# Experts' input copies on ScalarE, and weight loads tied to VectorE's place in the pass

## The chip, the cores and the metric

The kernel runs on one core of a Trainium2 chip. The metric is the device time of one execution in microseconds. Before the change, three runs gave 418.44, 418.54 and 419.1 us; the median is 418.54.

A core has five engines, each with its own queue of instructions: TensorE (PE; its weight loads are shown apart as PEld), VectorE (DVE), ScalarE (ACT), GpSimd (POOL) and the sync engine (SP). Engines wait for each other on semaphores. Data moves between HBM and the on-chip SBUF by DMA; the sync engine and POOL issue most of the transfers here. Matmul results go to PSUM, from where ScalarE or VectorE move them to SBUF.

## What is computed

An attention block with a gated state, then a mixture of 16 experts in 4 groups. Cut to what matters:

```python
# attention, per batch (4), head (8), step (768), head width 48
f = 1 / (1 + exp(-f_logit))
state = f[t] * state + outer(k[t], v[t])
y[t] = q[t] @ state
# rows of all heads side by side: x is 3072 x 384
g_idx = argmax(x @ w_group)            # group of 4
e_idx = argmax(x @ w_expert[g_idx])    # expert of 4 in the group
h  = maximum(x[tokens] @ w1[g, e], 0)  # 384 -> 1024
ye = h @ w2[g, e]                      # 1024 -> 384
out[tokens] = (g_softmax * e_softmax)[:, None] * ye
```

Every token goes to one of the 16 experts, so the tokens of an expert must be gathered before its matmuls and scattered after them.

## The kernel before

**Two stages.** Up to about 130 us the kernel works on the attention block in 12 units and, as chunks of tokens are done, ranks the experts by their number of tokens. It starts with two "early" passes, of the two fullest experts, for the tokens known by then. From about 154 us it runs 16 expert passes. Pass 0 and pass 15 take 128 rows each (the rest of the two early experts' tokens); passes 1 to 14 take 230 down to 174 rows (`WIDTHS`), one expert each, fullest first. `PLACES` maps the number of a pass to a place in the ranking, and `who` (one row of integers, made by VectorE at line 300) holds the expert's number for each place.

**One pass.** POOL gathers its rows (`fetch`, line 404, one indirect DMA for each block of up to 128 rows). The rows are turned so that the model dimension lies on the partitions. That is done in one of two ways:
- `square_in` (line 426): VectorE turns 32x32 squares from SBUF to SBUF. Passes 2 to 14 use it.
- `turn_in` (lines 435 to 441): TensorE transposes into PSUM (`xg_ps`), and a copy moves the result into the tile `xe`. The two early passes use it, with the copy on ScalarE, and passes 0, 1 and 15, with the copy on VectorE.

Then `up` (line 450) multiplies with the first layer, and ScalarE applies the relu from PSUM to SBUF (line 451). `down` (line 486, or `down_rows` at 471 for 128 rows) multiplies with the second layer; ScalarE moves the result from PSUM (487), VectorE turns it back in `square_out` (433), ScalarE scales the rows (458) and POOL scatters them to the output (461).

**Order of work.** For TensorE, VectorE, ScalarE and the sync engine, the program's order is the order of execution (`manual_schedule`, line 85); POOL's order is left to the scheduler. In the loop at lines 964 to 991, iteration n issues `square_out` of pass n-1, `square_in` of pass n+2, `up` of pass n+1 and `down` of pass n. On TensorE the order is therefore up(0), up(1), down(0), up(2), down(1), up(3), down(2) and so on to up(14), down(13), down(14), up(15), down(15). Iteration 2 ends with `beyond`, some bookkeeping on VectorE; iteration 3 ends with `weakest` and `flags`, where VectorE waits for one transpose by TensorE.

**Weights.** Each expert has two layers of 1536 KB. `load_weights` (line 395) has the sync engine read the expert's number into a register (388) and then issue the loads of the first and of the second layer (392). There are three sets of weight buffers: pool `wq` has one, used by passes 1, 4, 7 and so on; pool `wp` has two. A load waits until the matmuls of the pass that had the buffer before are through: pass m uses the buffers of pass m-3. The call stands at the end of iteration n and loads pass n+3 (984 and 985). During the attention stage, `load_next` (819) copies the number to another tile, `who_late`, before it is read.

Of the kernel before, what the change touches and what calls it, by code (L numbers as in the profile page):

```python
# [11 lines left out]
I32 = mybir.dt.int32  # L12
# [6 lines left out]
P = 128  # L19
# [4 lines left out]
def kernel(  # L24
# [12 lines left out]
    nc = tc.nc  # L37
# [5 lines left out]
    GE = G * EG  # L43
# [25 lines left out]
    wp = ctx.enter_context(tc.tile_pool(name="wp", bufs=2))  # L69
# [7 lines left out]
    def const(shape, dtype, name):  # L77
        return cp.tile(shape, dtype, tag=name, name=name)

    def bank(shape, name):  # L80
        return ps.tile(shape, FP32, tag="bank", name=name)
# [189 lines left out]
    who = const([1, GE], I32, "who")  # L271
# [115 lines left out]
    def value(ap, top):  # L387
        return nc.values_load(ap, engines=(ET.SP,), min_val=0, max_val=top, skip_runtime_bounds_check_because="a table that the routing makes within these bounds")

    def load_layer(pool, e, layer):  # L390
        w = pool.tile([P, KO, F] if layer == 1 else [P, FO, DM], FP32, tag=f"w{layer}", name=f"w{layer}")
        nc.sync.dma_start(out=w, in_=(w1v if layer == 1 else w2v)[bass.ds(e, 1)].rearrange("o p k f -> (o p) k f"))
        return w

    def load_weights(pool, ap):
        e = value(ap, GE - 1)
        return load_layer(pool, e, 1), load_layer(pool, e, 2)

    def fetch(pool, rows, n, top=N, late=False):

        w = {"n": n, "pool": pool, "early": top < N, "late": late, "blocks": [(j, min(P, n - j * P)) for j in range((n + P - 1) // P)]}
        w["x"] = pool.tile([P, len(w["blocks"]), RW], FP32, tag="xg", bufs=2 if pool is ep else 6, name="xg")
        for j, m in w["blocks"]:
            nc.gpsimd.indirect_dma_start(out=w["x"][:, j, :], out_offset=None, in_=x_dram[0:1 + top, :], in_offset=bass.IndirectOffsetOnAxis(ap=rows[:, j:j + 1], axis=0))  # L404
        return w

    def room(w, shape, name):

        full = w["pool"].tile([P, shape, P if w["pool"] is ep else WIDE], FP32, tag=name, name=name)
        w[name[:2].replace("xe", "xT") + "_full"] = full  # L410
        return full[:, :, 0:w["n"]]
# [9 lines left out]
    def square_in(w):  # L421

        w["xT"] = room(w, KO, "xe")
        x = w["x"][:, :, 0:DM].rearrange("p j (o g c) -> p j g o c", o=KO, c=SQ)
        xT = w["xT_full"].rearrange("p o (j k c) -> p j k o c", j=2, c=SQ)
        squares(w, lambda n, k_, rk, g, rg: nc.vector.transpose(out=xT[rg, 0:n, k_], in_=x[rk, 0:n, g]))  # L426

    def square_out(w):

        w["rows"] = w["pool"].tile([P, 2, DM], FP32, tag="yr", name="yr")  # L430
        y = w["rows"].rearrange("p j (o g c) -> p j g o c", o=KO, c=SQ)
        yT = w["yT_full"].rearrange("p o (j k c) -> p j k o c", j=2, c=SQ)
        squares(w, lambda n, k_, rk, g, rg: nc.vector.transpose(out=y[rk, 0:n, g], in_=yT[rg, 0:n, k_]))  # L433

    def turn_in(w):
        w["xT"] = room(w, KO, "xe")
        for j, m in w["blocks"]:
            pt = bank([P, KO, P], "xg_ps")
            for ko in range(KO):
                nc.tensor.transpose(out=pt[:, ko, 0:m], in_=w["x"][0:m, j, ko * P:(ko + 1) * P], identity=ident[0:m, 0:m])  # L440
            (nc.scalar.copy if w["early"] else nc.vector.tensor_copy)(w["xT"][:, :, j * P:j * P + m], pt[:, :, 0:m])  # L441

    def up(w, w1):
        n = w["n"]
# [31 lines left out]
    def down(w, w2):  # L476
        n = w["n"]
        if n == P:
            for _ in down_rows(w, w2):
                pass  # L480
            return
        w["yT"] = w["yT_full"][:, :, 0:n]
        for m in range(KO):
            yp = bank([P, n], "yo")
            for fo in range(FO):
                nc.tensor.matmul(yp, lhsT=w2[:, fo, m * P:(m + 1) * P], rhs=w["h"][:, fo, :], start=(fo == 0), stop=(fo == FO - 1))  # L486
            nc.scalar.copy(w["yT"][:, m, :], yp)  # L487

    def scaled(w, settle=False):
        if w["n"] > P:  # L490
            for j, m in w["blocks"]:
                with settled(settle and j):
                    put(w, j, m, w["rows"][:, j, :])
# [22 lines left out]
    def early():  # L516

        ws = [fetch(ep, rows_e[:, p:p + 1], P, (CLOSE + 1) * B * P) for p in range(EARLY)]
        yield
        for w in ws:  # L520
            turn_in(w)
            yield
        for p, w in enumerate(ws):
            yield from up(w, weights[p][0])
        for p, w in enumerate(ws):
            yield from down_rows(w, weights[p][1])
# [380 lines left out]
    wq = main.enter_context(tc.tile_pool(name="wq", bufs=1))  # L907
# [3 lines left out]
    PLACES = [0] + list(range(EARLY, GE)) + list(range(1, EARLY))  # L911

    def pass_of(n):
        p = PLACES[n]
        if p < EARLY:
            return fetch(mo, rows_p[:, p, 1:2], P)
        return fetch(mo, rows_p[:, p, :], WIDTHS[p - EARLY])

    fari = const([1, 1], I32, "fari")

    def weakest():

        worst = const([P, 1], FP32, "worst")
        nc.vector.tensor_reduce(out=worst, in_=decays.rearrange("p c a n -> p (c a n)"), axis=AX, op=OP.min)
        wt = bank([1, P], "wt")
        nc.tensor.transpose(out=wt, in_=worst, identity=ident)
        far = const([1, 2], FP32, "far")
        nc.vector.tensor_reduce(out=far[:, 0:1], in_=wt, axis=AX, op=OP.min)
        nc.vector.tensor_scalar(far[:, 1:2], far[:, 0:1], math.exp(-SAFE), None, OP.is_lt)
        nc.vector.tensor_copy(fari, far[:, 1:2])  # L930

    def flags():

        nc.vector.tensor_copy(both[:, 0:1], fari)
        nc.vector.tensor_scalar(rest, b_end, 0, None, OP.is_gt)
        nc.vector.tensor_tensor(both[:, 1:2], fari, rest, OP.max)
# [4 lines left out]
    ahead = {n: load_weights(wq if n % 3 == 1 else wp, who[0:1, PLACES[n]:PLACES[n] + 1]) for n in range(1, 2)}  # L941
# [8 lines left out]
    def run_up(n):  # L950
        for _ in up(ws[n], ahead[n][0]):
            pass

    outs = [const_out(i) for i in range(2)]
    turn_in(ws[0])
    for _ in first[0]:
        pass
    opening = up(ws[0], ahead[0][0])
    next(opening)
    next(opening)  # L960
    turn_in(ws[1])
    for _ in opening:
        pass
    for n in range(GE - 1):
        w = ws[n]
        if n + 3 < GE:
            ws[n + 3] = pass_of(n + 3)
        if n == 0:
            ahead[2] = load_weights(wp, who[0:1, PLACES[2]:PLACES[2] + 1])
        past, coming = ws.pop(n - 1, None), ws.get(n + 2)  # L970
        if past and past["n"] > P:
            square_out(past)
        if coming and coming["n"] > P:
            square_in(coming)
        if n + 2 < GE:
            run_up(n + 1)
        if past:

            scaled(past, n == GE - 3)
        if coming and coming["n"] == P:  # L980
            turn_in(coming)
        w["yT_full"] = outs[n % 2]
        down(w, ahead.pop(n)[1])
        if n + 3 < GE:
            ahead[n + 3] = load_weights(wq if n % 3 == 1 else wp, who[0:1, PLACES[n + 3]:PLACES[n + 3] + 1])
        if n == 2:
            with tc.tile_pool(name="tb", bufs=1) as tb:
                beyond(False, tb)
        if n == 3:
            weakest()  # L990
            flags()
# [79 lines left out]
    with tc.If(more > 0), ExitStack() as late:  # L1071
# [5 lines left out]
        with tc.For_i(0, last, 1) as i:  # L1077
# [14 lines left out]
            w = fetch(ep, row, P, late=True)  # L1092
# [32 lines left out]
```

## Time and profile before

| | |
|---|---|
| median of three runs | 418.54 us |
| the profiled execution | 417.84 us |
| its span, from the first to the last instruction | 416.0 us |
| mean granted TensorE clock | 0.994 |
| up(0), 128 columns, 48 matmuls | starts at 154.73 us |
| up(1), 230 columns, 48 matmuls | 164.32 us, takes 11.24 us |
| down(1), 230 columns, 48 matmuls | 189.56 us, takes 9.48 us |
| last matmul of down(15) ends | about 410.5 us |
| a weight layer, from issue to landing | 6.6 to 13.5 us, median 7.2 |
| line 441 on VectorE, four copies | 467 to 558 ns |
| line 441 on ScalarE, two copies | 479 and 480 ns |
| line 388, register load on the sync engine | 263 to 277 ns |

How to read the profile: it is one execution. Times are counted from the start of the span. A line of a timeline has a start, a length, the engine, the source line, the operation, the tile written and the tiles read, the shape and the number of like instructions merged; in brackets stand the engine's idle time before it and what ended that. A busy TensorE is one that has matmuls in its pipeline. "issue" stands for idle time in which nothing that the profile shows was waited for, "remote" for a release whose source was not found.

### The profile page before, as it was taken

The numbers are of one execution on the slowest core, as the hardware profiler recorded it, in microseconds if no ns is written. First come the engines' busy times: TensorE is split into PE (matmuls) and PEld (weight loads), VectorE is DVE, ScalarE is ACT, GpSimd is POOL, SyncE is SP. The second block draws the span as 40 slices with busy tenths as digits, with TensorE's granted clock in tenths as the row PEclk, the third lists the DMA queues.
The fourth block names the chain that finished last, engine by engine and source line by source line (L and its number), as shares of the span: only waits on it lengthen the run. The fifth ranks groups of instructions, "written<-read, shape, count | busy, mean of one in ns | idle before, by whom it ended". The sixth has DMA issues, their size and how long they took to land.

```text
span 416.0 us, 10268 instructions
## 1 busy us (share of the span) xinstructions
PE 404.0 (97%) x4143; PEld 371.9 (89%) x4143; DVE 264.3 (64%) x783; ACT 162.2 (39%) x365; POOL 85.7 (21%) x132
## 2 busy tenths in 40 slices
PE   8999999999999997999999999999999999999994
PEld 3888888888888966989999999999999999999992
DVE  6666878787998702440799767485595595584230
ACT  6777878887664211211223122222231232232220
POOL 5000010101040174001041221311321230120230
PEclk9999999999999999999999999999999999999999
DMA  9999987879869499855729467586495596485010
GB/s 191 208 216 197 201 179 147 164 159 289 244 225 378 163 337 345 318 179 184 271 84 335 137 245 265 164 315 208 170 348 169 217 352 200 173 318 162 28 48 24
DMA packets 132146, 88.99 MB, mean 214 GB/s; under 512 B 102582, under 2 KB 122748, under 8 KB 132090
## 3 DMA queue, kind: packets, MB, share of 16 engines
q1 hardware_dynamic: 125666, 75.50, 60.6%
q0 software_dynamic: 5792, 11.92, 9.5%
q10 hardware_dynamic: 632, 0.83, 0.6%
q8 instruction: 35, 0.57, 0.6%
q14 instruction: 21, 0.17, 0.1%
HBM read 78.71 MB, written 9.83 MB: 213 GB/s over the span
## 4 chain that ended last, share of the span: by engine, by line
PE 48%; issue 30%; DMA 9%; POOL 6%; DVE 3%; POOLq 1%; another core or an unknown queue 1%; ACT 1%; SPq 0%; ACTq 0%; DVEq 0%
PE hp L450 12%; PE yo L486 6%; DMA out_dram<-yt,xg 6%; PE yo L471 4%; PE cs L616 4%; POOL out_dram L461 4%; PE ap L704 3%; PE y L746 3%; POOL xg L404 2%; PE x_ps L795 2%; PE tr_q L650 2%; PE tr_k L650 2%; PE y L742 2%; PE ap L689 2%; PE y L754 2%
## 5 line engine op out<-in xcount | busy, mean ns | idle before, releaser
L450 PE MATMUL hp<-xe,w 128*128 128x128 f32 (+14 forms) x864 | 141.3, 323 | 2.6 <-issue 1.8
L450 PEld LDWEIGHTS hp<-xe,w 128*128 128x128 f32 x864 | 137.4, 192 | 4.5 <-issue 2.4
L486 PE MATMUL yo<-h,w 128*128 128x230 f32 (+13 forms) x672 | 115.8, 333 | 0.0
L433 DVE STREAM_TRANSPOSE yr<-yT 32x192 f32<-32x192 f32 (+1 forms) x208 | 70.5, 339 | 70.5 <-ACT yT L487 67.9
L486 PEld LDWEIGHTS yo<-h,w 128*128 128x128 f32 x672 | 113.7, 190 | 0.2
L451 ACT ACTIVATE h<-hp 128x256 f32<-128x256 f32 (+14 forms) x72 | 34.2, 478 | 109.1 <-PE hp L450 100.2
L426 DVE STREAM_TRANSPOSE xe<-xg 32x192 f32<-32x192 f32 (+1 forms) x208 | 69.6, 335 | 8.7 <-PE hp L450 5.8
L461 POOL DMA_INDIRECT out_dram<-yt,xg x32 | 34.5, 1078 | 156.1 <-ACT yt L458 150.5
L487 ACT COPY yT<-yo 128x230 f32<-128x230 f32 (+13 forms) x42 | 13.5, 325 | 80.5 <-PE yo L486 80.5
L404 POOL DMA_INDIRECT xg<-x_dram,rows_p x30 | 29.6, 986 | 51.1 <-DMA out_dram<-yt,xg 25.7
L471 PE MATMUL yo<-w,h 128*128 128x384 f32 x64 | 21.3, 486 | 0.0
L707 DVE TENSOR_TENSOR am<-ap,tri 128x512 f32<-128x512 f32 x24 | 15.1, 688 | 7.3 <-PE ap L704 7.3
L616 PE MATMUL cs<-ld_f,tri 128*128 128x384 f32 x48 | 18.5, 505 | 0.5 <-POOL blank L177 0.3
L471 PEld LDWEIGHTS yo<-w,h 128*128 128x128 f32 x64 | 11.9, 190 | 7.4
L458 ACT ACTIVATE yt<-yr,xg 128x384 f32<-128x384 f32 (+13 forms) x26 | 14.4, 604 | 5.4 <-DVE yr L433 5.4
L623 POOL DMA_DIRECT2D ends<-eq x10 | 5.4, 542 | 52.2 <-ACT eq L617 52.2
L692 DVE TENSOR_TENSOR am<-ap,seen 128x384 f32<-128x384 f32 x24 | 12.2, 551 | 5.5 <-PE ap L689 5.5
L757 ACT COPY xT<-y 128x512 f32<-128x512 f32 x24 | 13.4, 587 | 5.0 <-PE y L746 4.4
L651 ACT COPY Tk<-tr_k 128x512 f32<-128x512 f32 x24 | 15.2, 636 | 0.0
L651 ACT COPY Tq<-tr_q 128x512 f32<-128x512 f32 x24 | 15.0, 625 | 0.4 <-PE tr_q L650 0.3
L441 DVE COPY xe<-xg_ps 128x384 f32<-128x384 f32 (+1 forms) x4 | 2.1, 535 | 20.5 <-remote 9.7
L650 PE MATMUL tr_q<-ident,qh 128*128 128x128 f32 x96 | 14.5, 274 | 0.5 <-issue 0.5
(187 smaller groups left out, 448.4 us busy)
## 6 DMA issues: line engine op xcount, KB each, us to landing
w<-in_moe_w_dram SPq DMA_DIRECT2D x34, 1536.0 KB, 7.2
qh<-in_q_dram SPq DMA_DIRECT2D x12, 384.0 KB, 6.1
ld_k<-in_k_dram SPq DMA_DIRECT2D x12, 384.0 KB, 4.4
v<-in_v_dram SPq DMA_DIRECT2D x12, 384.0 KB, 5.4
ld_f<-in_f_logit_dram SPq DMA_DIRECT2D x11, 384.0 KB, 5.5
x_dram<-x_kept SPq DMA_DIRECT2D x2, 1536.0 KB
x_dram<-x POOLq DMA_DIRECT2D x2, 384.0 KB
x_dram<-x ACTq DMA_DIRECT2D x2, 384.0 KB, 7.4
```

The lines of the kernel that those rows point to most:

```text
L404: nc.gpsimd.indirect_dma_start(out=w["x"][:, j, :], out_offset=None, in_=x_dram[0:1 + top, :], in_offset=bass.IndirectOffsetOnAxis(ap=rows ...
L426: squares(w, lambda n, k_, rk, g, rg: nc.vector.transpose(out=xT[rg, 0:n, k_], in_=x[rk, 0:n, g]))
L433: squares(w, lambda n, k_, rk, g, rg: nc.vector.transpose(out=y[rk, 0:n, g], in_=yT[rg, 0:n, k_]))
L450: nc.tensor.matmul(hp[:, o, :], lhsT=w1[:, ko, (f + o) * P:(f + o + 1) * P], rhs=w["xT"][:, ko, :], start=(ko == 0), stop=(ko == KO - 1))
L451: nc.scalar.activation(h[:, f:f + 2, :], hp, AF.Relu)
L461: sent = nc.gpsimd.indirect_dma_start(out=out, out_offset=bass.IndirectOffsetOnAxis(ap=w["x"][0:m, j, DM + 1:RW].bitcast(U32), axis=0), in ...
L471: nc.tensor.matmul(yp, lhsT=w["h"][:, fo, :], rhs=w2[:, fo, :], start=(fo == 0), stop=(fo == FO - 1))
L486: nc.tensor.matmul(yp, lhsT=w2[:, fo, m * P:(m + 1) * P], rhs=w["h"][:, fo, :], start=(fo == 0), stop=(fo == FO - 1))
L616: nc.tensor.matmul(cs.rearrange("t h d -> t (h d)"), lhsT=tri, rhs=nl[:, b], start=True, stop=True)
L650: nc.tensor.transpose(out=pt[:, a, :], in_=w[nm + "h"][:, b, 2 * a:2 * a + 2, :].rearrange("t r d -> t (r d)"), identity=ident)
L651: nc.scalar.copy(w["T" + nm][:, b], pt)
L707: nc.vector.tensor_tensor(am[:, r], ap[r], tri.unsqueeze(1).broadcast_to((P, HP, P)), OP.mult)
```

## The change

First, the copy at the end of `turn_in`: ScalarE does it always, except in the block at the end of the program that handles tokens beyond the passes' widths (`late`). Second, the load of the weights: the call moves from the end of iteration n, for pass n+3, to the beginning of iteration n, for pass n+2, ahead of that iteration's `square_out` and `square_in`. VectorE copies the expert's number to a new tile, `who_next`, and the sync engine reads it from there. Pass 2's load, in iteration 0, stays as it is; the pools are the same for each pass.

```diff
-            (nc.scalar.copy if w["early"] else nc.vector.tensor_copy)(w["xT"][:, :, j * P:j * P + m], pt[:, :, 0:m])
+            (nc.vector.tensor_copy if w["late"] else nc.scalar.copy)(w["xT"][:, :, j * P:j * P + m], pt[:, :, 0:m])
...
+    who_next = const([1, GE], I32, "who_next")
...
         past, coming = ws.pop(n - 1, None), ws.get(n + 2)
+        if 0 < n < GE - 2:
+            p = PLACES[n + 2]
+            nc.vector.tensor_copy(who_next[:, p:p + 1], who[:, p:p + 1])
+            ahead[n + 2] = load_weights(wq if n % 3 == 2 else wp, who_next[0:1, p:p + 1])
         if past and past["n"] > P:
             square_out(past)
...
         down(w, ahead.pop(n)[1])
-        if n + 3 < GE:
-            ahead[n + 3] = load_weights(wq if n % 3 == 1 else wp, who[0:1, PLACES[n + 3]:PLACES[n + 3] + 1])
```

## The prediction

> **What bounds the kernel now.** I read three views: busy time by engine and by slice, then each engine's timeline around the places the change touches, then the same stretch cut into 5 us windows.
>
> ```profile
> PE 404.0 (97%) x4143; PEld 371.9 (89%) x4143; DVE 264.3 (64%) x783; ACT 162.2 (39%) x365; POOL 85.7 (21%) x132
> PE   8999999999999997999999999999999999999994
> ```
>
> TensorE is busy 404.0 of 416.0 us, and the slices show one dip in the middle, in slice 16 (about 156 to 166 us), where the first expert pass starts. Here are TensorE, ScalarE, VectorE and one issue of the sync queue in that place, each from its own timeline:
>
> ```profile
> 157.41 0.76 PE L440 MATMUL xg_ps<-ident,xg 128*128 128x128 f32 x6
> 158.00 1.97 PE L450 MATMUL hp<-xe,w 128*128 128x128 f32 x16
> 160.37 0.48 PE L450 MATMUL hp<-xe,w 128*128 128x128 f32 x2 [0.40 <-issue]
> 161.08 0.27 PE L450 MATMUL hp<-xe,w 128*128 128x128 f32 x1 [0.22 <-issue]
> 162.48 1.08 PE L450 MATMUL hp<-xe,w 128*128 128x128 f32 x5 [1.14 <-issue]
> 164.32 11.24 PE L450 MATMUL hp<-xe,w 128*128 128x230 f32 x48 [0.76 <-ACT h L451]
> ...
> 158.36 0.39 ACT L451 ACTIVATE h<-hp 128x256 f32<-128x256 f32 x1 [2.85 <-PE xg_ps L440]
> 163.23 0.94 ACT L451 ACTIVATE h<-hp 128x256 f32<-128x256 f32 x3 [4.48 <-remote]
> ...
> 163.28 0.94 DVE L441 COPY xe<-xg_ps 128x384 f32<-128x384 f32 x2 [9.67 <-remote]
> 164.14 5.70 DVE L426 STREAM_TRANSPOSE xe<-xg 32x192 f32<-32x192 f32 x16
> 175.60 5.71 DVE L426 STREAM_TRANSPOSE xe<-xg 32x192 f32<-32x192 f32 x16 [5.76 <-PE hp L450]
> ...
> 163.59 3.71 SPq L392 DMA_DIRECT2D w<-in_moe_w_dram  x1
> ```
>
> TensorE had run 16 matmuls of up(0) in 1.97 us, then needs from 160.0 to 163.6 for the last eight. ScalarE and VectorE both wake within 0.05 us of each other at 163.2, although the matmuls they need were issued by 158.2. I call this the stall. Only then does up(1) start.
>
> ```profile
> 155.00:160.00 5.00, 4.97 (x46) 4.78 (x44) 0.00 (x0) 0.90 (x2) 3.78 (x5) 1.00 1.04 328
> 160.00:165.00 5.00, 2.40 (x11) 1.89 (x12) 1.69 (x5) 0.94 (x3) 1.26 (x2) 0.99 1.00 338
> 165.00:170.00 5.00, 5.00 (x19) 4.54 (x18) 4.67 (x14) 0.56 (x1) 0.00 (x0) 0.67 1.04 401
> 170.00:175.00 5.00, 5.00 (x27) 4.90 (x26) 0.00 (x0) 1.11 (x2) 0.00 (x0) 1.00 0.80 308
> ```
>
> The columns are length, busy time of PE, PEld, DVE, ACT and POOL, granted clock, DMA share and GB/s. The DMA engines are full from 155 to 170 (share 1.00 to 1.04). After the stall the granted clock is 0.67 for one window, so up(1) takes 11.24 us where down(1), 48 matmuls of the same 230 columns, takes 9.48. From 170 us to the end of up(14) TensorE has no idle time. So only the handover at 160 to 168 us has anything to give back: 164.32 - 160.9 = 3.4 us of stall (eight matmuls at the usual 0.11 us would have ended at 160.9) and 11.24 - 9.48 = 1.8 us of slow clock, together 5.2 us.
>
> [...] the same 128x384 copy of line 441 takes 480 ns on ScalarE and 558 ns on VectorE, 78 ns apart. [...] 0.67 over 5 us is 3.3 us at half rate, directly after the stall[...]. [...] between 150 and 165 us the weights' queue holds 55.9% of them and POOL's gathers and scatters 46.2%, so a load issued later does leave room. [...] here line 388 takes 270 ns, and I use that.
>
> **The change, part by part.**
>
> *Copies moved to ScalarE.* In this run the four VectorE copies of line 441 move (one block of pass 0, two of pass 1, one of pass 15; the two early ones are on ScalarE already). VectorE loses 2.1 us; it is no bound, so that is worth nothing by itself.
> - Pass 0, at 153.05: ScalarE is idle from 150.02 to 154.93, so 0.48 replaces 0.56 us. Behind it waits the scaling of line 458, released only at 154.93. up(0) starts when the last matmuls of the early pass are through (154.7). Nothing.
> - Pass 1, at 163.28: ScalarE's order becomes relu 1, copy, copy, relu 2, relu 3. From 163.23: a relu occupies it 0.28 (three in 0.94), a 128x384 copy 0.48, the 102-row copy about 0.40. The copies would end near 164.4; VectorE's ended at 164.22. Behind them stand relus 2 and 3 of up(0), needed only by down(0) at 175.4, but up(1)'s first matmul is listed as released by a relu. If it needs the third one, which would move from 164.17 to about 164.95, the loss is 0.7 us. Bounds: below, 0 (or a gain of no more than 0.08 a copy[...]); above, 0.7. I take 0.1, because the last relu and the last VectorE copy ended 0.05 us apart and the copy was later.
> - Pass 15, at 384.84: ScalarE works off two scalings from 384.87 to 385.98 and then waits until 387.36; the copy fits, and up(15) reads it at 399. Nothing. If that cover were gone, 0.48 us of delay would still have 13 us of room.
>
> *Loads behind a copy.* Thirteen loads (passes 3 to 15) leave "who" and get a 1x1 integer VectorE copy each: 131 ns by the like copy of line 819 (97 to 364), 13 x 0.131 = 1.7 us of VectorE, spread. What it does is move the issue: the copy for pass m stands behind the input transposes of pass m-1. With 0.13 for the copy, 0.27 for the register load and some 0.1 for sequencing, the first layer's load is issued 0.5 us after VectorE gets there. VectorE's free points come from its timeline, before's issue from the sync queue's, need from the start of up(m):
> - pass 3: free 169.84, so issue 170.3 instead of 163.59; needed 198.88
> - pass 4: free 181.31, so 181.8 instead of about 181.6; needed 216.56
> - pass 5: free 219.96 (behind the 18 operations of "beyond", 211.42 to 219.96), so 220.4 instead of about 199.9; needed 233.95
> - pass 6: free 235.20 (behind "weakest" and "flags", which wait for TensorE), so 235.7 instead of about 217.6; needed 250.99
> - pass 7: free 246.57, so 247.1 instead of about 234.9; needed 267.71
> - pass 15: free 373.53, so 374.0 instead of about 363.3; needed about 399.1
>
> A load lands in 6.6 to 13.5 us, median 7.2. The sync queue then takes the second layer, which waits for down(m-3) as before or goes at once. Pass 5 is the narrowest: 220.4 + 7.2 = 227.6 against 233.95; with 13.5 it is 233.9, just in time. Pass 6 has 15.3 us. All others have 20 us or more. Behind the waiting register load nothing stands on the sync queue except the next weights; behind the copy on VectorE stand the output and input transposes of the iteration, later by 0.13 us, whose tightest user, up(5), has 233.95 - 231.3 = 2.6 us of room. POOL's queue keeps its place; gathers and scatters meet fewer weights in their first microseconds, but TensorE waits for none of them after 164 us. So the load part costs 0, and up to 0.3 if pass 5 lands at the slow end.
>
> *The stall itself.* Everything issued before 163.59 stays: both layers of passes 1 and 2, eleven gathers, two scatters. The first load that moves, pass 3, was issued after the stall was over. So I expect it to stay. The trace doesn't show its cause, so its bounds are wide: a gain of 5.2 us if it goes, a loss of about 2.4 if it grows.
>
> *Sum.* 0.1 - 0 + 0 = +0.1 us on the span: 416.1. The profiled execution took 417.84 for its span of 416.0, and the median of the runs, 418.54, is 0.70 above that. 416.1 + 1.84 + 0.70 = 418.6.
>
> **The rivals.**
> - *The stall shrinks or goes.* For it: it falls in the only stretch with a full DMA, ScalarE and VectorE wait in it for the very hand-overs that the change rearranges, and a pass-3 load no longer adds to the traffic that up(1) meets. Against it: nothing that moves lies ahead of its end. Gone altogether: 418.5 - 5.2 = 413.3; shortened by half with the slow window kept: 418.5 - 1.7 = 416.8; I put the case at 415.5.
> - *The hand-over on ScalarE gets longer.* up(1) waits for the relus behind the copies, 0.7 us[...]. 418.5 + 2.4 = 420.9. [...] For it: the release named for 164.32 is ScalarE. Against: relu 2 and 3 feed only down(0).
> - *Weights of pass 5 come late.* If they need 18 us, as under the full DMA at 145 to 170 us seems possible, TensorE waits 4 us at 233.95[...]: 424.2. It decides from 14.4 us on. Against it: by 220 us the earlier weights have landed.
> - *The part with the loads does nothing at all*, since TensorE never waited for a weight: this is the forecast without the 0.1, 418.5.
>
> **How the numbers follow.** Forecast with the fourth case: 0.44. Stall shrinks: 0.35. ScalarE hand-over: 0.15. Pass 5 late: 0.06. The likeliest time is 418.6, with its own range 418.1 to 419.3 (0 to 0.7 us of hand-over, and the spread of the three runs, 418.44 to 419.1). A change of 0.2%, 0.8 us, is about what a measurement of this kernel can tell from none. So faster 0.35, same 0.44, slower 0.21. For eight in ten the range goes down to 414.8, which leaves out a stall that goes altogether (0.12), and up to 420.9, which leaves out late weights and a little more (0.07).
>
> **What would show it.** Right: the stretch from 158 to 164 us on TensorE with eight slow matmuls and a window at about 0.67 after it, line 441 six times on ScalarE and never on VectorE, pass 3's load at about 170 and pass 5's at about 220, and no idle TensorE from 170 us on. Wrong: up(1) starting before 163 or after 165, idle time of TensorE at 233.95 or 250.99, or POOL's gathers in another order with a different landing of pass 1's rows.

## The result and the profile after

The changed kernel takes 421.09 us, median of six runs (419.47 to 421.88), against 418.51 for the kernel before in the same comparison (417.83 to 419.45): 1.006 times as long, 95% interval 1.0039 to 1.008. The forecast was 418.6 us, no change.

The profiled execution of the changed kernel took 419.47 us with a span of 417.6. It was the fastest of the six; the other five took 420.93 to 421.88 us. First the page of the kernel after, the two lines that answer to those shown of before:

```profile
PE 404.2 (97%) x4143; PEld 371.7 (89%) x4143; DVE 264.4 (63%) x792; ACT 164.4 (39%) x369; POOL 85.9 (21%) x132
PE   7999999999999998999999999999999999999994
```

TensorE's work is the same. VectorE has nine instructions more: 13 new small copies less the four that went to ScalarE. The dip of TensorE stands in the same slice, the 16th (about 157 to 167 us here). Its timeline, then ScalarE's and VectorE's in that place, of the kernel after:

```profile
161.54 2.08 PE L450 MATMUL hp<-xe,w 128*128 128x128 f32 x17
163.83 0.99 PE L450 MATMUL hp<-xe,w 128*128 128x128 f32 x4 [0.21 <-issue]
165.27 0.59 PE L450 MATMUL hp<-xe,w 128*128 128x128 f32 x3 [0.45 <-issue]
167.82 9.59 PE L450 MATMUL hp<-xe,w 128*128 128x230 f32 x48 [1.96 <-ACT xe L441]
...
166.70 0.38 ACT L451 ACTIVATE h<-hp 128x256 f32<-128x256 f32 x1 [5.31 <-PE hp L450]
166.98 0.79 ACT L441 COPY xe<-xg_ps 128x384 f32<-128x384 f32 x2
167.64 0.69 ACT L451 ACTIVATE h<-hp 128x256 f32<-128x256 f32 x2
...
172.85 0.14 DVE L974 COPY who_next<-who 1x1 int32<-1x1 int32 x1
177.50 5.71 DVE L426 STREAM_TRANSPOSE xe<-xg 32x192 f32<-32x192 f32 x16 [4.51 <-issue]
```

The stall is there as before, and it begins and ends 3.5 us later: the run of matmuls of up(0) that it breaks off starts at 161.54 instead of 158.00, and up(1) at 167.82 instead of 164.32. So the time was lost ahead of it. A single line tells how far ahead: line 300, where VectorE writes the experts' numbers at the end of the attention stage. Its instructions in the kernel before, then after, with "first and last start" in the middle:

```profile
L300 DVE CAST who<-names x2: 157/159/161, 106.8 to 143.7; 1x2 int32<-1x2 f32 x1, 1x16 int32<-1x16 f32 x1
```

```profile
L300 DVE CAST who<-names x2: 159/161/163, 110.3 to 147.2; 1x2 int32<-1x2 f32 x1, 1x16 int32<-1x16 f32 x1
```

The attention stage ends 3.5 us later, at 147.2 instead of 143.7 us, and it was 3.5 us behind already at 110. Not one of its instructions is touched by the diff. Following one copy of ScalarE, line 772, unit by unit through that stage, the kernel after is behind by 0.96 us at 22.8 us, 1.43 at 66.2, 2.47 at 76.3, 3.01 at 86.5, 3.63 at 96.6, and by 3.5 from 119 us to the end of the stage (times of the kernel before). A delay that grows through the stage points at something each unit needs: its loads. The DMA queue of the sync engine, with packets, MB and share of 16 engines over the whole span, of the kernel before and then after:

```profile
q1 hardware_dynamic: 125666, 75.50, 60.6%
```

```profile
q1 hardware_dynamic: 125666, 75.50, 67.4%
```

Same packets, same bytes, 11% more time in them (67.4 / 60.6, over nearly equal spans). The windows of 0 to 95 us show where; before, then after (columns as in the windows shown earlier, the last two DMA share and GB/s):

```profile
0.00:30.00 30.00, 27.92 (x380) 20.62 (x380) 20.38 (x58) 21.26 (x44) 6.59 (x46) 1.00 1.02 203
30.00:60.00 30.00, 29.45 (x680) 25.28 (x679) 21.94 (x57) 24.27 (x53) 2.56 (x5) 1.00 0.94 190
60.00:95.00 35.00, 34.98 (x813) 30.00 (x814) 27.41 (x80) 29.83 (x70) 2.73 (x6) 1.00 0.83 167
```

```profile
0.00:30.00 30.00, 27.68 (x372) 19.83 (x373) 19.93 (x58) 20.67 (x42) 6.60 (x46) 1.00 1.18 176
30.00:60.00 30.00, 29.17 (x676) 25.02 (x675) 21.35 (x53) 23.90 (x52) 2.56 (x5) 1.00 1.14 180
60.00:95.00 35.00, 33.22 (x747) 29.01 (x748) 25.80 (x73) 27.76 (x65) 2.71 (x6) 1.00 1.13 176
```

Before, the DMA engines have room from 60 us on (share 0.83), and TensorE is busy for 34.98 of the 35 us up to 95. After, they stay full (1.13 to 1.18; over 1, so the times of some packets overlap), move fewer bytes a second in the first 60 us, and TensorE loses 1.8 us between 60 and 95 us. In the packet records, the 192-byte packets by which q, k, v and f arrive (one row of one head) took 15.2 ns on average before and 19.9 after, up to 95 us: before, 99 of 100 take 15 ns or less; after, a quarter take 24 ns or more and one in twenty 36 or more.

What could touch those loads? The new tile. `who_next` takes 64 bytes of each partition in the pool of constants, which lies ahead of all others, so every later tile moved up by 64 bytes in SBUF. The rows of q and v go to tiles padded to 64 numbers a head, that is one 192-byte row every 256 bytes. Take a *line* to be 256 bytes of a partition that start at a multiple of 256. In the built programs v's first tile lies at byte 162336 of each partition before and at 162400 after. So before, every row starts 32 bytes into a line and ends at 224; after, it starts at 96 and runs 32 bytes into the next line. Rows of f and k are packed, 192 bytes apart. That the engines work more slowly on the moved tiles is not what the two pages show: VectorE is busy for 264.3 us before and 264.4 after, TensorE for 404.0 and 404.2, and the 2.2 us that ScalarE has more are about the four copies that it took over. That gave the theory to test, the *place theory*, against the *edit theory*, that the copies or the loads themselves cost the time.

### The profile page after: what moved, and what is told of

It is laid out like the page before. It is cut to its first block, busy times and chain, and to the rows that moved or that the text cites. A ratio compares the mean times of both kernels' runs of the same rounds, so it can differ in the third digit from the quotient of the medians.

```text
span 417.6 us, 10278 instructions
## 1 busy us (share of the span) xinstructions
PE 404.2 (97%) x4143; PEld 371.7 (89%) x4143; DVE 264.4 (63%) x792; ACT 164.4 (39%) x369; POOL 85.9 (21%) x132
## 3 DMA queue, kind: packets, MB, share of 16 engines
q1 hardware_dynamic: 125666, 75.50, 67.4%
## 4 chain that ended last, share of the span: by engine, by line
PE 48%; issue 30%; DMA 8%; POOL 6%; DVE 2%; SPq 2%; POOLq 1%; ACT 1%; DVEq 0%
PE hp L450 13%; DMA out_dram<-yt,xg 7%; PE yo L486 6%; PE yo L471 4%; POOL out_dram L461 4%; PE cs L616 3%; PE y L754 3%; PE x_ps L795 2%; POOL xg L404 2%; SPq L591 2%; PE ap L689 2%; PE y L746 2%; PE tr_k L650 2%; PE y L742 2%; PE ds L722 2%
## 5 line engine op out<-in xcount | busy, mean ns | idle before, releaser
L450 PE MATMUL hp<-xe,w 128*128 128x128 f32 (+14 forms) x864 | 139.5, 320 | 2.7 <-ACT xe L441 2.0
L450 PEld LDWEIGHTS hp<-xe,w 128*128 128x128 f32 x864 | 136.0, 190 | 4.3 <-ACT xe L441 2.2
L650 PE MATMUL tr_k<-ident,kh 128*128 128x128 f32 x96 | 14.4, 274 | 0.5 <-DVE kh L639 0.5
```

What stands on the lines that cost most here:

```text
L450: nc.tensor.matmul(hp[:, o, :], lhsT=w1[:, ko, (f + o) * P:(f + o + 1) * P], rhs=w["xT"][:, ko, :], start=(ko == 0), stop=(ko == KO - 1))
L650: nc.tensor.transpose(out=pt[:, a, :], in_=w[nm + "h"][:, b, 2 * a:2 * a + 2, :].rearrange("t r d -> t (r d)"), identity=ident)
```

## The experiments

All kernels of a group ran on one chip, and each is compared with the kernel before on that chip; the groups ran on different chips. The first group's kernel before has a median of 418.19 us, the second's 412.49 and the third's 412.21, so only ratios are set against each other across groups. Ratios and intervals are those on record; they are near the quotients of the two medians and not the same (for e2_pad64 the medians give 1.0066).

### First group: the change without the shift, and the shift without the change

```diff
e1_aligned, on the kernel after
-    who_next = const([1, GE], I32, "who_next")
+    who_next = const([1, 4 * GE], I32, "who_next")
e2_pad64, on the kernel before (e4_pad32 has 8 in place of 16)
+    pad = const([1, 16], I32, "pad")
+    nc.gpsimd.memset(pad, 0)
e3_copies, on the kernel before
-            (nc.scalar.copy if w["early"] else nc.vector.tensor_copy)(...)
+            (nc.vector.tensor_copy if w["late"] else nc.scalar.copy)(...)
```

Expected of e1_aligned: 

> The whole change, with who_next made 256 bytes long instead of 64, so that every later tile lies 256 bytes further on instead of 64. Place theory (the loss comes from where the attention tiles lie): 192-byte packets back to 15 ns, who written near 143.7 us, time 418.0 to 418.8. Edit theory (the moved copies or loads cost the time): as the changed kernel, 421 us. No theory expects the stall at 160 us to go.

Measured: 417.85 us, ratio 1.0005 (0.9988 to 1.0022), packets 15.3 ns, `who` written at 144.4 us. The whole change, with the tiles back in their place within a 256-byte line, costs nothing that this comparison can tell from none (0.2%).

Expected of e2_pad64: 

> The kernel before, with one unused tile of 64 bytes in the pool of constants and nothing else. Place theory: as slow as the changed kernel, 420.5 to 421.5 us, with 192-byte packets of 15, 24 and 36 ns and a mean near 20. Edit theory: 418.5 us and 15 ns.

Measured: 420.94 us, ratio 1.0082 (1.0059 to 1.0106), packets 19.9 ns, again with a quarter at 24 ns or more and one in twenty at 36 or more, `who` at 147.0. An unused tile of 64 bytes has the whole loss. The edit theory falls with these two. Line 300 and the sync queue of e1_aligned, then of e2_pad64:

```profile
L300 DVE CAST who<-names x2: 157/159/161, 107.4 to 144.4; 1x2 int32<-1x2 f32 x1, 1x16 int32<-1x16 f32 x1
q1 hardware_dynamic: 125666, 75.50, 60.4%
```

```profile
L300 DVE CAST who<-names x2: 157/160/163, 110.0 to 147.0; 1x2 int32<-1x2 f32 x1, 1x16 int32<-1x16 f32 x1
q1 hardware_dynamic: 125666, 75.50, 66.9%
```

Expected of e3_copies: 

> The kernel before with the copies on ScalarE alone; no tile moves. Place theory: 418.5 to 419.0, the hand-over at up(1) 0 to 0.3 us later. Edit theory with the copies to blame: 420 us or more, up(1) over 1 us later.

Measured: 418.16 us, ratio 0.9999 (0.9982 to 1.0016), packets 15.3 ns.

Expected of e4_pad32: 

> The kernel before with an unused tile of 32 bytes. If 192-byte rows of q and v that run over a 256-byte line are what costs: those rows now end exactly on the line (64 to 256), so 15 ns for them and at most a small loss from f and k, 418.5 to 419.3 us. If any shift off the old place costs: 420 us or more. If the places don't matter: 418.5.

Measured: 418.13 us, ratio 1.0003 (0.9984 to 1.0023), packets 16.2 ns, `who` at 143.7. A shift as such shows no loss, and neither do rows of q and v that end exactly on the line.

### Second group: whose rows, and which line

```diff
e5_qv_only, on the kernel before: moves the pool of q and v (and of the tiles made from them) alone by 64 bytes
+        hole = fp.tile([P, 16], I32, tag="hole", name="hole")
+        nc.gpsimd.memset(hole[0:1], 0)
e6_fk_only, on the kernel before: a like tile of 64 bytes ahead of f and k (pool sb), and hole with 48
+        gap = sb.tile([P, 16], I32, tag="gap", bufs=1, name="gap")
+        nc.gpsimd.memset(gap[0:1], 0)
e7_pad128: as e2_pad64, with 32 in place of 16
```

Expected of e5_qv_only: 

> The kernel before, with an unused 64-byte tile that moves only the padded tiles of q and v (and the tiles made from them) by 64 bytes; f, k and the weights stay. If rows of q and v that run over a 256-byte line are the cause: the whole loss, 420.5 to 421.5 us, mean of the 192-byte packets 19 to 20 ns. If it is f and k, or the weights: 418.2 us and 15 ns.

Measured: ratio 1.0074 (1.0056 to 1.0091), packets 20.0 ns, `who` at 147.1.

Expected of e6_fk_only: 

> The kernel before, with only f, k and the working tiles of the attention stage moved by 64 bytes, and q and v by 256. If q and v are the cause: 418.2 us, 15 ns. If f and k are: 420 us or more.

Measured: ratio 0.9997 (0.9986 to 1.0009), packets 15.3 ns, `who` at 143.2. So it is not the move of f and k. Whether other starts of their rows would cost, this run can't say: moved by 64 bytes, packed rows still start at 0, 64, 128 and 192 in turn. The times in microseconds expected for these two don't apply on this chip; the ratios do. The DMA view from 0 to 95 us of e5_qv_only and then of e6_fk_only, with the KB of an issue and the median us to landing:

```profile
q1 hardware_dynamic: 86618, 16.50, 113.6%
...
qh<-in_q_dram SPq DMA_DIRECT2D x11, 384.0 KB, 6.9
ld_k<-in_k_dram SPq DMA_DIRECT2D x11, 384.0 KB, 6.3
ld_f<-in_f_logit_dram SPq DMA_DIRECT2D x10, 384.0 KB, 6.8
v<-in_v_dram SPq DMA_DIRECT2D x10, 384.0 KB, 7.0
```

```profile
q1 hardware_dynamic: 91347, 17.40, 91.5%
...
qh<-in_q_dram SPq DMA_DIRECT2D x11, 384.0 KB, 4.4
ld_k<-in_k_dram SPq DMA_DIRECT2D x11, 384.0 KB, 4.4
ld_f<-in_f_logit_dram SPq DMA_DIRECT2D x11, 384.0 KB, 5.5
v<-in_v_dram SPq DMA_DIRECT2D x11, 384.0 KB, 5.2
```

Moving q and v alone slows all four, whose loads the sync engine issues (SPq) and which make up nearly all of its queue (q1): a load lands in 6.3 to 7.0 us instead of 4.4 to 5.5.

Expected of e7_pad128: 

> The kernel before with an unused tile of 128 bytes: rows of q and v start 160 bytes into a 256-byte line and run 96 bytes into the next. If the 256-byte line counts: slow, 420.5 to 421.5 us, packets near 20 ns. If only the place within 128 bytes counts, which is the same as before: 418.2 us, 15 ns.

Measured: ratio 1.0067 (1.0048 to 1.0086), packets 19.6 ns. The place within 128 bytes is the one of before, the place within 256 is not: it is the 256-byte line that counts.

### Third group: the other starts within the line

These repeat e5_qv_only with 24, 40 and 48 numbers in `hole` in place of 16. Each has only two or three executions.

Expected of e9_qv128: 

> The kernel before, with q and v alone moved by 96 bytes: rows start 128 bytes into a 256-byte line, a multiple of 64, and run over its end. If running over the line is enough: slow, packets 19 to 20 ns and 0.7% more time. If it takes a start that is no multiple of 64 as well (rows of f and k run over lines at multiples of 64 and take 15 ns): 15 ns and no loss.

Measured: ratio 1.0079 (1.0057 to 1.0102), packets 19.4 ns. Running over the line is enough; the start may be a multiple of 64 or not.

Expected of e10_qv192: 

> As the one before, with rows of q and v at 192 bytes into a line, a multiple of 64, running over its end by 128 bytes. Line alone: slow. Line and odd start: 15 ns and no loss.

Measured: ratio 1.0094 (1.007 to 1.0119), packets 19.4 ns.

Expected of e11_qv224: 

> As the one before, with rows of q and v at 224 bytes into a line, no multiple of 64, running over its end by 160 bytes. Both theories: slow, packets 19 to 20 ns, 0.7% more time. If this one is fast, neither is right.

Measured: ratio 1.0082 (1.0058 to 1.0105), packets 19.6 ns. All starts together, from the packet records up to 95 us of each profiled execution:

| start of a q or v row in its 256-byte line | runs over | mean of the 192-byte packets | ratio |
|---|---|---|---|
| 32 (before, e1, e3, e6) | no | 15.2 to 15.3 ns | 0.9997 to 1.0005 |
| 64 (e4) | no, ends on it | 16.2 ns | 1.0003 |
| 96 (after, e2, e5) | by 32 bytes | 19.9 to 20.0 ns | 1.006 to 1.0082 |
| 128 (e9) | by 64 | 19.4 ns | 1.0079 |
| 160 (e7) | by 96 | 19.6 ns | 1.0067 |
| 192 (e10) | by 128 | 19.4 ns | 1.0094 |
| 224 (e11) | by 160 | 19.6 ns | 1.0082 |

### Two runs on the stall, which tell nothing of its cause

The prediction's largest rival was about the stall at 160 us. To empty the DMA engines at that moment, e8_late2 and e12_late2_again put the load of pass 2 behind the input transposes of that pass:

```diff
+    who_next = const([1, 4 * GE], I32, "who_next")
...
-        if n == 0:
-            ahead[2] = load_weights(wp, who[0:1, PLACES[2]:PLACES[2] + 1])
...
             square_in(coming)
+        if n == 0:
+            p = PLACES[2]
+            nc.vector.tensor_copy(who_next[:, p:p + 1], who[:, p:p + 1])
+            ahead[2] = load_weights(wp, who_next[0:1, p:p + 1])
```

Expected of e8_late2: 

> The kernel before, with the load of pass 2 alone behind a copy by VectorE that follows the input transposes of pass 2 (near 170 us instead of 146 and 155), in a tile of 256 bytes. If the stall at 160 us comes of weights and gathers filling the DMA engines together: the stall shrinks or goes, up(1) starts near 161 to 162 us, 413.5 to 416.5 us, if pass 2's weights then land before up(2), 17 us after up(1)'s start. If the stall has another cause: 418.2 us, and more if the weights land late.

Expected of e12_late2_again: 

> The kernel before, with the load of pass 2 alone behind a VectorE copy near 170 us. Where the kernel before shows the stall at 160 us: if it comes of a full DMA at that moment, up(1) starts 2 to 3 us earlier and the time is 1 to 5 us less; if not, no change. Where the kernel before shows no stall: no change.

Measured: ratios 1.0002 (0.9993 to 1.0012) and 1.0005 (0.9991 to 1.002). But on these chips there was no stall to remove. TensorE's timeline of e6_fk_only, whose expert stage is that of the kernel before:

```profile
156.90 0.76 PE L440 MATMUL xg_ps<-ident,xg 128*128 128x128 f32 x6
157.49 12.19 PE L450 MATMUL hp<-xe,w 128*128 128x128 f32 x72
169.51 5.32 PE L471 MATMUL yo<-w,h 128*128 128x384 f32 x16
```

and its windows, then those of e8_late2:

```profile
155.00:160.00 5.00, 5.00 (x48) 5.00 (x47) 0.94 (x2) 1.15 (x4) 3.83 (x4) 1.00 1.01 321
160.00:165.00 5.00, 5.00 (x29) 4.90 (x28) 4.45 (x13) 0.94 (x2) 1.00 (x1) 1.00 1.00 367
165.00:170.00 5.00, 5.00 (x27) 4.77 (x26) 1.35 (x5) 1.40 (x3) 0.00 (x0) 1.00 1.05 404
```

```profile
155.00:160.00 5.00, 5.00 (x47) 5.00 (x47) 0.94 (x2) 1.15 (x3) 3.79 (x4) 1.00 1.03 362
160.00:165.00 5.00, 5.00 (x29) 4.90 (x28) 4.50 (x13) 0.94 (x2) 1.01 (x1) 1.00 0.32 118
165.00:170.00 5.00, 5.00 (x26) 4.75 (x25) 1.49 (x6) 1.45 (x3) 0.00 (x0) 1.00 0.39 108
```

The edit did what it says: the DMA share falls from 1.00 to 0.32. But in e6_fk_only TensorE runs up(0) and up(1) without a gap although the DMA engines are as full as where the stall was seen. So a full DMA is not enough for it. The profiles of before and after and all four of the first group have the stall; none of the eight of the other two groups has it. It goes with the chip, or with something else in which these groups differ, and not with the kernel. What it is stays open.

## Why the prediction was wrong

**The step that failed** is the one that said "Everything issued before 163.59 stays: both layers of passes 1 and 2, eleven gathers, two scatters", and with it the sum "0.1 - 0 + 0 = +0.1 us on the span". What is issued did stay. Where it lands in SBUF did not. The line `who_next = const(...)` was in the diff and was given no term; it costs 3.5 us of the profiled attention stage and 0.6 to 0.8% of the time (1.006 here, 1.0082 in e2_pad64). e2_pad64 shows it alone, e1_aligned shows the change without it. The prediction's own sign of being wrong, up(1) starting after 165, came true, but for this reason and not for the hand-over that it had in mind.

**The terms that were priced came out as priced.**
- The copies: e3_copies, 0.9999. At the hand-over up(1) starts 20.20 us after the first matmul of the early passes' second layer (147.62 to 167.82), before 20.24 (144.08 to 164.32). The 0.1 us is not seen, and would be too small to see. The 0.7 us for relus behind the copies did not come: up(1) is released by the copy, and relus 2 and 3 follow it. (The 0.08 us a copy that the prediction names as the most to gain is the 78 ns between 558 and 480 ns in the trace of before.)
- The loads: pass 3 was forecast at 170.3 and pass 5 at 220.4; with the delay from the attention stage added (3.5 us at the first; 1.9 at the second, as the slow clock after the stall had by then cost the kernel before 1.65 us and not the kernel after) that is 173.8 and 222.3. The sync queue of the kernel after has

```profile
173.50 0.37 SPq L392 DMA_DIRECT2D w<-in_moe_w_dram  x1
222.35 1.00 SPq L392 DMA_DIRECT2D w<-in_moe_w_dram  x2
```

A layer now lands in a median 9.2 us, not 7.2; the longest is 10.0, not 13.5. That comes of the edit and not of the place (10.1 in e1_aligned, 7.3 in e2_pad64), probably since both layers are now often issued together, as in the second line. up(5) starts at 235.79 with no idle time. The forecast of 131 ns for a small copy met 142.
- The stall: forecast to stay, and it did, on the chip of these two profiles. The slow clock after it, in before a granted clock of 0.50 from 164.9 to 168.3 us, did not show in the profiled execution after (up(1) 9.59 us instead of 11.24), which gave 1.65 us back. That looks like luck of the execution: between 165 and 170 us the granted clock was 0.67 in before and 0.50 in e1_aligned and e4_pad32, but 1.00 in after and e3_copies, with the stall in all five. The profiled execution has the highest mean clock of its six (0.997; the others 0.991 to 0.995) and is the fastest. So 3.5 us lost in the stage are 1.6 us in the span. Why they are 2.6 in the medians is not shown; on the two chips without the stall it is 3.1 to 3.9 us.

**The rivals.** "The hand-over on ScalarE gets longer" had 420.9 us for its time, close to the measured 421.09, but that is chance: its mechanism did not occur. Its 2.4 us and the 424.2 us for late weights each count 1.7 us for a further stretch of slow clock after a longer wait. That was the author's estimate: the stretch behind the stall in before, 3.4 us at 0.50, costs such a 1.7 us, but that a wait brings one is not shown, and after and e3_copies have the stall without it. Pass 5 was not late. The stall did not shrink. The case that came true, one outside the stage that the diff speaks of, was not among them. It could have been: the share of the DMA engines in the attention stage, 1.02 and 0.94 in its first two windows, shows a stage with no room for slower loads, and the edit puts a tile ahead of all of that stage's tiles.

**What it means for the change.** Its two parts as meant are worth nothing that can be measured (1.0005, 0.9988 to 1.0022), since TensorE, outside the stall, waits neither for VectorE's copies nor for weights (in before it is busy for all of the 225 us from 170 to 395). No version tried here beats the kernel before.

## What to carry to other kernels

A new tile can move every tile allocated after it (one of 64 bytes did here, and the attention stage ended 3.5 us later); when a time changes in a stage that the diff doesn't touch, compare the time in its DMA packets at equal counts and bytes (here 60.6% and 67.4%), and then the addresses. Rows of 192 bytes loaded every 256 gave a mean packet of 15.2 to 16.2 ns here when each lay within one 256-byte line and of 19.4 to 20.0 when it ran over: where a kernel loads such rows, try the start of the tile, and fix it rather than leaving it to what happens to lie ahead. Before calling an edit neutral, change its footprint as e1_aligned does, to 256 bytes instead of 64, and measure that too (1.0005, where the edit as it stood had 1.006): it takes one run to part the edit from the move.

## What was not expected of the hardware

- With 192-byte rows written every 256 bytes (q and v, half of all such packets), the mean over all these packets is 15.2 to 16.2 ns when those rows stay within a 256-byte line and 19.4 to 20.0 when they run over. The mean follows whether a row lies in one line or in two. How far it runs over, 32 to 160 bytes, made no clear difference: from a start of 96 to one of 224 the mean doesn't rise (19.9 to 20.0, then 19.6 ns). Why running over costs time is not shown.
- The packed rows of f and k, 192 bytes apart, run over a line in two cases of four before, and still take 15 ns (99 of 100 of all 192-byte packets of before take no more). With three of four running over (e4_pad32) the mean over all packets is only 16.2; which rows have that 1 ns is not known, as q and v moved too. Why packed rows are spared is open; packing q and v was not tried.
- The DMA cost grew far more than the time: in 95 us the queue's packets went from 90.7% to 113% of that time on 16 engines, some 21 us an engine, of which 3.5 reached the end of the stage. Packet times overlap (the 113%), and the loads of a unit are issued two units ahead; how much either hides was not measured.
- The stall, some 5 us with its slow clock by the prediction's sum, went with the chip (or what else differed there) and not with the kernel: 418.2 us for the kernel before on a chip whose profiles have it, 412.2 and 412.5 on two others whose profiles don't.
